# Gated attention and MLP on one core: keys on GpSimd's queue, SP in text order, and six-head turns at the end of the attention

## The chip, the core and the metric

The kernel runs on one core of one Trainium2 chip. A core has five engines with queues of their own: TensorE (PE: matmuls; PEld is its weight load), VectorE (DVE), ScalarE (ACT), GpSimd (POOL) and SyncE (SP), which here only issues DMAs. DMAs issued by SP and by GpSimd move data between HBM and the on-chip memory. Matmul results land in eight PSUM banks of 128 partitions by 512 fp32 numbers. The metric is the device time of one execution in microseconds (us); lower is better.

## What is computed

The input x has 2048 tokens of 448 features. Two blocks are computed from the same x and mixed per token by a gate:

```python
qkv = x @ wqkv                       # 16 heads of 28
p = softmax(q @ k.T * 28 ** -0.5)    # per head, 2048 x 2048
a = (p @ v) @ wo
y = layernorm(x)
b = gelu(y @ w1 + b1) @ w2 + b2      # 448 -> 1792 -> 448
g = sigmoid((x * gate_w).sum(-1))
out = g * a + (1 - g) * b
```

## The kernel before

Precision: most fp32 products are made from a high and a low part (`wh`/`wl`, `xh`/`xl`, `hl[:,0]`/`hl[:,1]`, ...). ACT copies the high part, DVE or POOL subtracts it from the raw value to get the low part, and three matmuls (high-high, high-low, low-high) go into one bank.

The work has three stages.

1. The projection stage (lines 138 to 301). For each of four token chunks `c` of 512, seven feature tiles `qk_tile(c, m)` of q and k and four token tiles `v_tile` are made. Each q/k tile is evicted by ACT (L190) and DVE (L191) into one of three buffers `hl` and stored to the HBM array `qk` (L192, 512 KB). Each value tile is evicted by ACT (L206) into one of three buffers `vt` and stored to `vs` (L208). Between these, the LayerNorm of the first chunk is prepared for the MLP (`ln_fetch`, `ln_apply`: two POOL operations, ACT's L131, one more POOL operation), and in chunk 3 the first seven tiles of w1 are loaded (L95) and split (L100, L103). In this stage only PE runs in the order of the text; for SP, ACT, DVE and POOL a planner chooses the order, and may let instructions of the next stage pass those of this one.

2. The MLP stage (from L557). For each chunk, 14 tiles `mlp1(c, f)` (11 matmuls at L529, two gelus at L532 and L533 on ACT, a subtraction on POOL at L534), then four tiles `mlp2(c, i)` (42 matmuls at L542, L543, L547). `mlp1` uses banks 0 and 1 in turn, so tile f needs the gelus of tile f-2 to be done. In chunk 0 the other seven tiles of w1 and all of w2 are fetched through four staging buffers, copied by ACT and subtracted: `low_w1` by POOL (L103), `low_w2` by DVE (L113). Between the MLP's matmuls a `filler` puts "row maxima": score matmuls of 28 rows (L362) into banks 2 to 7, whose maximum DVE takes (L342, L344). They give the softmax its shift. They read the keys of four heads, `khr` (L425, four DMAs of 224 KB), and queries `qd` (L319). Here all engines run in text order.

3. The attention stage (from L751). The 16 heads are four groups of four; 16 steps `n` = (group, chunk), each with 16 key tiles of four heads, 1024 "heads" (units) in all. They go in turns of U = 5 units: a triple of score products into banks 0 to 2 (nine matmuls, L483), an exponential of 1536 columns on ACT (L488), a pair into banks 3 and 4 and its exponential, then the value products (`pv_mm`, L746, four units to a step of four) of the key tiles that are complete, into bank 7. The units of a triple sit in different 32-row strips of PE. Up to three row-maximum matmuls per turn go into banks 5 and 6. When all 1040 row-maximum pieces are done, the turns go on without them. After each step but the last `finish` normalises the result in pieces at turns `STEPS` after the step's end; for the last group it ends with four projections (`project`, twelve matmuls at L651 to L653 in bank 6).

SP issues its DMAs in order: an issue that waits for a semaphore holds up all behind it.

Of the kernel before, what the change touches and what calls it, by code (L numbers as in the profile page):

```python
# [15 lines left out]
P = 128  # L16
S = 2048
# [17 lines left out]
W1, W2 = 0.233, 0.205  # L35
LQ = 12
STEPS = (2, 5, 7, 8, 9, 10)


@with_exitstack  # L40
def kernel(ctx: ExitStack, tc: tile.TileContext, xt, wqk, wv, wo, xk, w1, b1, w2, b2,
# [67 lines left out]
    def high_w2(f):  # L109
        nc.scalar.activation(w2h[f], wraw[2, f], AF.Copy)  # L110

    def low_w2(f):
        nc.vector.tensor_sub(w2l[f], wraw.pop((2, f)), w2h[f].bitcast(F32))  # L113

    yh, yl = (my.tile([P, n, CH], F32R, name=f"y{n}") for n in (4, 3))
    lnr = my.tile([P, 2, CH], F32, name="lnr")
# [10 lines left out]
    def ln_apply(c, t):  # L127
        x = lnx.pop((c, t))
        nc.gpsimd.tensor_sub(x, x, lnr[:, 0])
        nc.gpsimd.tensor_mul(x, x, lnr[:, 1])  # L130
        nc.scalar.activation(yh[:, t], x, AF.Copy)  # L131
        if t < 3:
            nc.gpsimd.tensor_sub(yl[:, t], x, yh[:, t].bitcast(F32))
        else:
            nc.gpsimd.tensor_sub(yh[64:128, t], x[64:128], yh[64:128, t].bitcast(F32))


    with tc.tile_pool(name="qx", bufs=2) as qx, tc.tile_pool(name="qo", bufs=3) as qo, \
# [106 lines left out]
            split_x(0, t)  # L245
        load_wqk(1)
        for c in range(NC):
            for m in range(NM):
                if c == 0:
                    if m + 2 < NM:  # L250
                        load_wqk(m + 2)
                    if m == 1:
                        for v in vt:
                            nc.gpsimd.memset(v[:, :, DH:DH + 1], 1.0)
                            nc.gpsimd.memset(v[:, :, DH + 1:32], 0.0)
                    if m == 3:
# [160 lines left out]

    khi = dict.fromkeys(range(MLP_G + 1), khr)

    def load_khr(g, k=None):  # L420

        sl = slice(0, S) if k is None else slice(k * CH, (k + 1) * CH)
        for j in range(4):
            r = D + (4 * g + j) * DH
            nc.sync.dma_start(khr[32 * j:32 * j + DH, sl].bitcast(F32), qk[0, r:r + DH, sl])  # L425

    def load_khi(g):
        if g == MLP_G:
# [40 lines left out]
        nc.sync.dma_start(qs[n][0][DH:P:32].bitcast(F32), ms[g][:, c * CH:(c + 1) * CH])  # L469

    U, UA = 5, 3
    probs = {}

    def scores(units, most, tiles):

        def product(u, i):
# [4 lines left out]
            nc.tensor.matmul(bank[:, u % U], a[r, k * P:(k + 1) * P], b[r], start=(i == 0), stop=(i == 2))  # L483

        def exps(units):
            t = tiles(len(units))
            b = units[0] % U
            nc.scalar.activation(t, bank[:, b:b + len(units)], AF.Exp, scale=SCALE)  # L488
            for i, u in enumerate(units):
                probs[u] = t[:, i]  # L490

        first, last = units[:UA], units[UA:]
        if most > 0:
            filler.max.issue(5, 1, [(first[0] + 3) % 4])
        for i in range(3):
            for u in first:
                product(u, i)
        exps(first)
        for i in range(3):
            for u in last:  # L500
                product(u, i)
            if i == 0 and most > 1:
                filler.max.issue(6, 1, [(first[0] + 1) % 4, (first[0] + 2) % 4])
        if last:
            exps(last)
        if most > 2:
            filler.max.issue(5, 1, [(first[0] + 1) % 4, (first[0] + 2) % 4])


    ml = ExitStack()  # L510
# [43 lines left out]
        nc.sync.dma_start(gbs[c * TPC + i], gb)  # L554

    E = mybir.EngineType
    with tc.manual_schedule(engines={E.SP, E.Pool, E.Activation, E.DVE}):  # L557

        order = [x for i in range(7) for x in (NF + 7 + i, i)] + list(range(7, NF))
        def high(k):  # L560
# [2 lines left out]
        def low(k):  # L563
            low_w2(k) if k < NF else low_w1(k - NF, nc.gpsimd)

        def stage(f):

            return order[max(0, 3 * (f - 1) // 2 - 1):max(0, 3 * f // 2 - 1)]

        for c in range(NC):  # L570
            for f in range(NF):
                if c == 0:
                    if f == 0:
                        stages += [lnr[:, 0], lnr[:, 1]]
# [12 lines left out]
            if c == 0:  # L587
                for k in stage(NF - 1):
                    low(k)
                for k in order[3 * (NF - 1) // 2 - 1:]:  # L590
                    high(k)
                    low(k)
                stages[2:] = []
            if c == NC - 1:
                m0.close()
# [4 lines left out]
                def early(n):  # L600
# [150 lines left out]
    with tc.manual_schedule(engines={E.SP, E.Pool, E.Activation, E.DVE}):  # L751
# [2 lines left out]
        ready = 0  # L754
        at = -1
        since = 0
        for u in range(0, 4 * steps, U):
            units = list(range(u, min(u + U, 4 * steps)))
            while at < units[-1] // 4:
                at += 1  # L760
                n, k = divmod(at, NT)
# [34 lines left out]
            ready = (units[-1] + 1) // 4  # L796
            since += 1
            if ended:
                n = summed // NT - 1
                fin, since = finish(n // NC, n % NC, pv), 0  # L800
                next(fin)
            elif fin is not None and since in STEPS:
                next(fin, None)
        while summed < steps:
            pv_mm(summed)
            summed += 1
# [54 lines left out]
```

## Time and profile before

| | us |
|---|---|
| median of 3 runs (lowest, highest) | 1138.23 (1138.23, 1141.04) |
| the profiled execution's own time | 1140.1 |
| its span, first to last instruction | 1138.3 |
| PE busy | 1114.2 |
| DVE busy | 739.6 |
| ACT busy | 633.9 |
| POOL busy | 327.2 |

Times in the profile are microseconds from the start of the span. A row of the timeline gives the start, the busy time, the engine, the line of the kernel, the operation, what it writes and reads, the count of merged instructions, and in brackets the idle time before it and who ended it. A row of the windows gives busy time (and count) of PE, PEld, DVE, ACT and POOL in a stretch, then PE's granted clock, the busy share of the DMA engines and the rate in GB/s. SPq is SP's queue of DMA issues.

### The profile page before, as it was taken

The page shows a single profiled execution, that of the slowest core. Times are in us where ns is not written, and L with a number is a line of the kernel's source. Part 1 is how long each engine was busy: PE and PEld are TensorE (multiplying, and loading weights), DVE is VectorE, ACT ScalarE, POOL GpSimd, SP SyncE. Part 2 cuts the span into 40 slices and gives each one's busy share as a digit, 9 for nine tenths or more (in the row PEclk, how much of TensorE's full clock was granted, in tenths as well). Part 3 has the DMA queues.
Part 4 walks back from the last instruction along what each step waited for, and adds up shares of the span by engine and source line. Part 5 has one row for each costly group of instructions (what it writes and reads, how often), then busy time and mean ns, then how long its engine had stood idle before and what let it go on. Part 6 is the DMA issues. An engine that isn't in the chain of part 4 may idle for free.

```text
span 1138.3 us, 19785 instructions
## 1 busy us (share of the span) xinstructions
PE 1114.2 (98%) x8136; PEld 678.9 (60%) x8136; DVE 739.6 (65%) x1031; ACT 633.9 (56%) x668; POOL 327.2 (29%) x348
## 2 busy tenths in 40 slices
PE   7999799999999999999999999999999999999996
PEld 6888677777767777744444444444444444464554
DVE  4443298888888888576666666666766766644102
ACT  5333460231131142188787887877878787747652
POOL 4006373344333332013112221221222125425140
PEclk9999899999999999999999999999999999999998
DMA  7996542010220105063100220012111102021201
GB/s 235 302 302 231 203 119 72 26 46 18 67 54 18 43 9 128 28 161 90 28 18 19 61 73 18 20 27 52 48 34 36 28 13 89 12 64 39 67 26 41
DMA packets 53055, 84.35 MB, mean 74 GB/s; under 512 B 8492, under 2 KB 28476, under 8 KB 52052
## 3 DMA queue, kind: packets, MB, share of 16 engines
q1 hardware_dynamic: 48900, 77.19, 22.5%
q0 software_dynamic: 4064, 5.89, 2.2%
q8 instruction: 64, 1.05, 0.4%
q14 instruction: 27, 0.22, 0.1%
HBM read 56.40 MB, written 26.49 MB: 73 GB/s over the span
## 4 chain that ended last, share of the span: by engine, by line
PE 94%; DMA 2%; DVE 1%; ACT 1%; issue 0%; SPq 0%; POOL 0%; ACTq 0%; DVEq 0%
PE bank L746 22%; PE bank L483 21%; PE bank L362 15%; PE bank L529 12%; PE bank L188 6%; PE bank L547 4%; PE bank L542 4%; PE bank L543 4%; PE bank L204 2%; PE bank L651 1%; PE bank L652 1%; PE bank L653 1%; DMA qk<-hl 1%; DMA raw<-in_xt 0%; DVE mx L344 0%
## 5 line engine op out<-in xcount | busy, mean ns | idle before, releaser
L488 ACT ACTIVATE pt<-bank 128x1536 f32<-128x1536 f32 (+1 forms) x408 | 482.3, 1234 | 151.5 <-PE bank L483 142.6
L342 DVE TENSOR_REDUCE mx<-bank 128x1 f32<-128x512 f32 x618 | 409.7, 687 | 175.5 <-PE bank L362 162.7
L746 PE MATMUL bank<-pt,vg 128*32 128x512 f32 x2038 | 260.9, 602 | 0.0
L344 DVE TENSOR_REDUCE mx<-bank 128x2 f32<-128x1024 f32 x203 | 238.8, 1219 | 32.5 <-PE bank L362 32.5
L362 PE MATMUL bank<-khi,qd 28*128 28x512 f32 x512 | 240.7, 479 | 0.1
L362 PEld LDWEIGHTS bank<-khi,qd 28*128 28x128 f32 x512 | 92.3, 181 | 148.1 <-DVE mx L342 105.0
L483 PE MATMUL bank<-qh,klo 28*128 28x512 f32 x1024 | 177.5, 393 | 0.0
L529 PE MATMUL bank<-y,w1f 128*128 128x512 f32 x616 | 154.1, 401 | 6.4 <-ACT h L533 6.4
L483 PE MATMUL bank<-qh,khi 29*128 29x512 f32 x768 | 160.0, 480 | 0.2 <-ACT pt L488 0.2
L529 PEld LDWEIGHTS bank<-y,w1f 128*128 128x128 f32 x616 | 113.5, 190 | 42.1 <-issue 12.3
L483 PE MATMUL bank<-ql,khi 28*128 28x512 f32 x768 | 132.3, 390 | 0.0
L534 POOL TENSOR_TENSOR hl<-h,hh 128x512 fp32r<-128x512 f32 x56 | 73.1, 1307 | 133.7 <-ACT h L533 93.0
L746 PEld LDWEIGHTS bank<-pt,vg 128*32 128x32 f32 x2038 | 45.5, 108 | 84.1 <-issue 83.3
L483 PEld LDWEIGHTS bank<-qh,klo 28*128 28x128 f32 x1024 | 89.1, 185 | 4.1
L532 ACT ACTIVATE hh<-bank,b1s 128x512 fp32r<-128x512 f32 x56 | 38.6, 689 | 88.3 <-PE bank L529 88.2
L553 ACT ACTIVATE h<-bank 128x448 f32<-128x448 f32 x16 | 8.7, 546 | 141.5 <-PE bank L547 107.5
L547 PE MATMUL bank<-w2h,hl 128*128 128x448 f32 x224 | 85.6, 382 | 0.0
L483 PEld LDWEIGHTS bank<-qh,khi 29*128 29x128 f32 x768 | 62.2, 181 | 37.6 <-ACT pt L488 33.0
L542 PE MATMUL bank<-w2h,hh 128*128 128x448 f32 x224 | 84.0, 375 | 0.0
L667 POOL DMA_DIRECT2D lt<-ob x15 | 11.0, 736 | 252.3 <-DVE ob L666 252.3
L543 PE MATMUL bank<-w2l,hh 128*128 128x448 f32 x224 | 82.5, 368 | 0.0
L362 PE MATMUL bank<-khr,qd 28*128 28x512 f32 x512 | 79.8, 466 | 1.5 <-DVE mx L344 1.5
(113 smaller groups left out, 1243.7 us busy)
## 6 DMA issues: line engine op xcount, KB each, us to landing
qk<-hl SPq DMA_DIRECT2D x28, 512.0 KB
raw<-in_xt SPq DMA_DIRECT2D x16, 256.0 KB
vs<-vt SPq DMA_DIRECT2D x16, 256.0 KB
s<-in_xt SPq DMA_DIRECT2D x16, 256.0 KB
rc<-rls POOLq DMA_DIRECT2D x60, 64.0 KB, 2.2
bxr<-in_xk SPq DMA_DIRECT2D x8, 448.0 KB
gbs<-h SPq DMA_DIRECT2D x16, 224.0 KB
klo<-qk SPq DMA_DIRECT2D x16, 224.0 KB
```

The source lines that it names most:

```text
L188: nc.tensor.matmul(ps, a, b, start=(i == 0), stop=(i == len(ops) - 1))
L342: nc.vector.reduce_max(self.mx[:, c0:c0 + 1], bank[:, b0], axis=AX)
L344: nc.vector.reduce_max(self.mx[:, c0:c1 + 1:c1 - c0], bank[:, b0:b1 + 1], axis=AX)
L362: nc.tensor.matmul(bank[:, b], self.qds[self.n][r, i * P:(i + 1) * P], khi[self.n // NC][r, k * 512:(k + 1) * 512], start=True, stop=True)
L483: nc.tensor.matmul(bank[:, u % U], a[r, k * P:(k + 1) * P], b[r], start=(i == 0), stop=(i == 2))
L488: nc.scalar.activation(t, bank[:, b:b + len(units)], AF.Exp, scale=SCALE)
L529: nc.tensor.matmul(ps, a, b, start=(i == 0), stop=(i == len(ops) - 1))
L534: nc.gpsimd.tensor_sub(hl[f], h, hh[f].bitcast(F32))
L542: nc.tensor.matmul(a, hh[f][:, sl], w2h[f], start=(f == 0), stop=False)
L543: nc.tensor.matmul(a, hh[f][:, sl], w2l[f], start=False, stop=False)
L547: nc.tensor.matmul(a, hl[f][:, sl], w2h[f], start=False, stop=(f == NF - 1))
L746: nc.tensor.matmul(pv[32 * j:32 * j + 32, :], vg[n // NC][:, k, 32 * j:32 * j + 32], probs.pop(4 * step + j), start=(k == 0), stop=(k == N ...
```

## The change

There are four parts.

- SP is put in text order from the last chunk of the projection stage on (before: from the start of the MLP stage).
- The keys `khr` of the first group are loaded on GpSimd's queue, called one `mlp1` tile earlier in the text (f = 0 instead of 1).
- At the end of chunk 0 of the MLP, the last three high parts of w2 are made first, and of the last four `low_w2` the second and fourth go to GpSimd instead of VectorE.
- In the attention, once all row maxima are done, turns have six units (two triples, banks 0 to 5), and the value products that are ready go between the two triples, except those of the last complete key tile. The second triple's exponentials go into three tiles that held keys (`khi0`, `khr`, `khi2`). The pieces of `finish` come at turns `LSTEPS`.

```diff
+LSTEPS = (2, 4, 6, 7, 8, 9)
...
-    def low_w2(f):
-        nc.vector.tensor_sub(w2l[f], wraw.pop((2, f)), w2h[f].bitcast(F32))
+    def low_w2(f, lo=nc.vector):
+        lo.tensor_sub(w2l[f], wraw.pop((2, f)), w2h[f].bitcast(F32))
...
         for c in range(NC):
+            if c == NC - 1:
+                texts.enter_context(tc.manual_schedule(engines={mybir.EngineType.SP}))
...
-    def load_khr(g, k=None):
+    def load_khr(g, k=None, queue=nc.sync):
...
-            nc.sync.dma_start(khr[32 * j:32 * j + DH, sl].bitcast(F32), qk[0, r:r + DH, sl])
+            queue.dma_start(khr[32 * j:32 * j + DH, sl].bitcast(F32), qk[0, r:r + DH, sl])
...
-    with tc.manual_schedule(engines={E.SP, E.Pool, E.Activation, E.DVE}):
+    with texts, tc.manual_schedule(engines={E.Pool, E.Activation, E.DVE}):
...
-                    if f == 1:
-                        load_khr(0)
+                    if f == 0:
+                        load_khr(0, queue=nc.gpsimd)
...
-                for k in stage(NF - 1):
-                    low(k)
-                for k in order[3 * (NF - 1) // 2 - 1:]:
+                rest = order[3 * (NF - 1) // 2 - 1:]
+                for k in rest:
                     high(k)
-                    low(k)
+                for n, k in enumerate(stage(NF - 1) + rest):
+                    low_w2(k, nc.gpsimd if n % 2 else nc.vector)
...
         exps(first)
+        if between:
+            between()
...
-        for u in range(0, 4 * steps, U):
-            units = list(range(u, min(u + U, 4 * steps)))
+        while u < 4 * steps:
+            if not late and filler.done >= NG * NC * 65:
+                late = [(mpool.tile([P, S], F32, name="khr", bufs=1) if g == MLP_G else
+                         aq.tile([P, S], F32, name=f"khi{g}")) for g in range(NG - 1)]
+            units = list(range(u, min(u + (UL if late else U), 4 * steps)))
...
+            def values(upto):
+                nonlocal summed, ended
+                while summed < upto and not ended:
+                    pv_mm(summed)
+                    summed += 1
+                    ended = summed % NT == 0
+
+            def pt(n, p):
+                if late and p:
+                    late.append(late.pop(0))
+                    return late[-1][:, :n * CH].rearrange("p (n c) -> p n c", c=CH)
+                return ap.tile([P, n, CH], F32, name=f"pt{n}")
+
             if u:
-                scores(units, min(3, filler.due()), lambda n: ap.tile([P, n, CH], F32, name=f"pt{n}"))
-            ended = False
-            while summed < ready and not ended:
-                pv_mm(summed)
-                summed += 1
-                ended = summed % NT == 0
+                scores(units, min(3, filler.due()), pt, (lambda: values(ready - 1)) if late else None)
+            values(ready)
```

In the changed program the orders of the engines near the end of the projection stage are these. SP issues the seven `qk` stores of chunk 3, each followed by one load (the LayerNorm's fourth input tile after the first, then w1 tiles), then the four `vs` stores, then the `qd` loads, then the staged weight loads. Before, three of the four `qd` loads stood ahead of the first of these stores, the fourth `qd` load, three staged weight loads and the first `khr` load between them, and the other `khr` loads between the `vs` stores or right behind them. ACT evicts the first three q/k tiles of chunk 3 before the first split of w1 and before the fourth LayerNorm copy, and the other four in turn with w1 splits. Before, all seven stood behind the fourth LayerNorm copy. POOL issues the four `khr` loads between the w1 subtractions of tiles 2, 4 and 5.

More of the change, by code (lines that the diff above doesn't have):

```diff
@@ L135, in ln_apply @@
             nc.gpsimd.tensor_sub(yh[64:128, t], x[64:128], yh[64:128, t].bitcast(F32))
+    texts = ExitStack()
     with tc.tile_pool(name="qx", bufs=2) as qx, tc.tile_pool(name="qo", bufs=3) as qo, \
@@ L471, with scores, product @@
     U, UA = 5, 3
+    UL = 6
     probs = {}
-    def scores(units, most, tiles):
-        def product(u, i):
+    def scores(units, most, tiles, between=None):
+        def product(p, i):
+            u = units[p]
             n, k, j = u // 4 // NT, u // 4 % NT, u % 4
@@ L482, in product, with exps @@
             r = slice(32 * j, 32 * j + r)
[L483 to L492, printed above, removed]
+            nc.tensor.matmul(bank[:, p], a[r, k * P:(k + 1) * P], b[r], start=(i == 0), stop=(i == 2))
+        def exps(at):
+            t = tiles(len(at), at[0])
+            nc.scalar.activation(t, bank[:, at[0]:at[-1] + 1], AF.Exp, scale=SCALE)
+            for i, p in enumerate(at):
+                probs[units[p]] = t[:, i]
+        first, last = list(range(len(units)))[:UA], list(range(len(units)))[UA:]
         if most > 0:
-            filler.max.issue(5, 1, [(first[0] + 3) % 4])
+            filler.max.issue(5, 1, [(units[0] + 3) % 4])
         for i in range(3):
-            for u in first:
-                product(u, i)
+            for p in first:
+                product(p, i)
         exps(first)
+        if between:
+            between()
         for i in range(3):
-            for u in last:
-                product(u, i)
+            for p in last:
+                product(p, i)
             if i == 0 and most > 1:
-                filler.max.issue(6, 1, [(first[0] + 1) % 4, (first[0] + 2) % 4])
+                filler.max.issue(6, 1, [(units[0] + 1) % 4, (units[0] + 2) % 4])
         if last:
@@ L506, in scores @@
         if most > 2:
-            filler.max.issue(5, 1, [(first[0] + 1) % 4, (first[0] + 2) % 4])
+            filler.max.issue(5, 1, [(units[0] + 1) % 4, (units[0] + 2) % 4])
     ml = ExitStack()
@@ L598, with early @@
                 first = {3: aq.tile([P, S], F32, name="klo", bufs=2), 2: aq.tile([P, NT, P], F32, name="vg", bufs=2)}
-                def early(n):
+                def early(n, p):
                     t = first[n] if n == 3 else first[n].rearrange("p a b -> p (a b)")
@@ L756 @@
         since = 0
-        for u in range(0, 4 * steps, U):
-            units = list(range(u, min(u + U, 4 * steps)))
+        u = 0
+        late = []
+        while u < 4 * steps:
[3 more added lines that the diff above has]
+            units = list(range(u, min(u + (UL if late else U), 4 * steps)))
             while at < units[-1] // 4:
@@ L788 @@
                         load_v(g + 1)
-            if u:
-                scores(units, min(3, filler.due()), lambda n: ap.tile([P, n, CH], F32, name=f"pt{n}"))
-            ended = False
-            while summed < ready and not ended:
-                pv_mm(summed)
-                summed += 1
-                ended = summed % NT == 0
+            ended = False
+            def values(upto):
[9 more added lines that the diff above has]
+                return ap.tile([P, n, CH], F32, name=f"pt{n}")
+            if u:
+                scores(units, min(3, filler.due()), pt, (lambda: values(ready - 1)) if late else None)
+            values(ready)
             ready = (units[-1] + 1) // 4
@@ L799 @@
                 n = summed // NT - 1
-                fin, since = finish(n // NC, n % NC, pv), 0
+                fin, since, when = finish(n // NC, n % NC, pv), 0, LSTEPS if late else STEPS
                 next(fin)
-            elif fin is not None and since in STEPS:
+            elif fin is not None and since in when:
                 next(fin, None)
+            u = units[-1] + 1
         while summed < steps:
```

## The prediction

> **What bounds the kernel now.** I read the page's busy lines and slices first, then the chain, then the timelines of PE, ACT, SP and DVE where the slices of PE dip.
>
> ```profile
> span 1138.3 us, 19785 instructions
> PE 1114.2 (98%) x8136; PEld 678.9 (60%) x8136; DVE 739.6 (65%) x1031; ACT 633.9 (56%) x668; POOL 327.2 (29%) x348
> PE   7999799999999999999999999999999999999996
> PE 94%; DMA 2%; DVE 1%; ACT 1%; issue 0%; SPq 0%; POOL 0%; ACTq 0%; DVEq 0%
> ```
>
> TensorE is busy 98% of the span and 94% of the chain. So a change helps in two ways only: it fills a hole of PE, or it takes PE work away. Leaving out the first and last slices, which the change does not touch, the one dip is the fifth slice, 114 to 142 us.
>
> ```profile
> 117.25 5.18 PE L529 MATMUL bank<-y,w1f 128*128 128x512 f32 x22
> 128.59 4.29 PE bank L529 x11
> 122.40:128.60 6.20, 0.04 (x2) 0.01 (x1) 0.16 (x1) 3.15 (x5) 0.00 (x0) 0.71 0.97 343
> 128.60:132.90 4.30, 4.30 (x12) 3.44 (x13) 0.85 (x1) 2.08 (x4) 2.52 (x2) 0.63 0.48 103
> ```
>
> PE does the MLP's first two tiles (22 matmuls from 117.25, 0.235 us each) to 122.42 and then stands until 128.59: 6.17 us. The third tile's 11 matmuls then take 4.29 us instead of 11 x 0.235 = 2.59, at a clock of 0.63: 1.70 us more. Who held PE? The third tile needs bank 0, so the first gelu. ACT's and SP's rows before it:
>
> ```profile
> 102.82 0.63 ACT L131 ACTIVATE y<-s 128x512 fp32r<-128x512 f32 x1 [4.73 <-POOL s L130]
> 105.34 0.59 ACT L190 ACTIVATE hl<-bank 128x512 fp32r<-128x512 f32 x1
> 116.67 0.60 ACT L190 ACTIVATE hl<-bank 128x512 fp32r<-128x512 f32 x1 [3.89 <-DMA qk<-hl]
> 119.61 1.41 ACT L206 ACTIVATE vt<-bank 128x448 f32<-128x448 f32 x3
> 125.42 0.54 ACT L206 ACTIVATE vt<-bank 128x448 f32<-128x448 f32 x1 [4.39 <-DMA vs<-vt]
> 125.98 1.28 ACT L532 ACT_TABLE_LOAD   x1
> 119.03 0.32 SPq L425 DMA_DIRECT2D khr<-qk  x1
> 122.66 1.12 SPq L425 DMA_DIRECT2D khr<-qk  x1
> ```
>
> ACT begins the seven evictions of chunk 3 only at 105.34, behind the LayerNorm copies. With three buffers they run at the pace of the stores (waits on the DMA). The last value eviction waits for a store to 125.42; the table load and two gelus follow. From there to PE's start it is 128.59 - 125.42 = 3.17 us. SP meanwhile issues key loads between the stores.
>
> **Part by part.**
>
> *SP in text order, keys on GpSimd.* In the changed order three q/k evictions and two value evictions stand right behind ACT's third LayerNorm copy, and SP issues no staged weight load and no `qd` load before the last value store. When does the last value eviction start?
>
> ```profile
> 97.02 0.63 ACT L131 ACTIVATE y<-s 128x512 fp32r<-128x512 f32 x1 [4.04 <-POOL s L130]
> 105.00:110.00 5.00, 5.00 (x24) 4.29 (x23) 4.03 (x6) 2.72 (x6) 2.76 (x2) 1.00 0.62 213
> 110.00:115.00 5.00, 5.00 (x27) 4.58 (x26) 1.70 (x3) 0.90 (x2) 0.00 (x0) 1.00 1.01 323
> qk<-hl SPq DMA_DIRECT2D x8, 512.0 KB
> raw<-in_w SPq DMA_DIRECT2D x4, 256.0 KB
> khr<-qk SPq DMA_DIRECT2D x4, 224.0 KB
> ```
>
> The third copy ends at 97.65; two value evictions (about 0.5 each) and a q/k eviction with its subtraction bring the first store to about 99.5. From there to the store that the last eviction waits for, 7 x 512 KB go to `qk`, 7 x 256 KB come from w1, one 256 KB LayerNorm tile and the first 256 KB value store move, and two key loads of 224 KB: 6336 KB, 6.5 MB. At 323 to 343 GB/s (the stretches with a DMA share near 1) that takes 19 to 20 us, to 118.5 to 119.6. At 213 GB/s it is 30.5 us, to 130.0. I take 120.5, one us behind the first, since the DMA engines were only 0.62 busy at the low rate: there they lacked work. PE then goes on at 120.5 + 3.17 = 123.7: gain 4.9. Best: the gelu is there by 122.42, gain 6.17. Worst: 133.2, a loss of 4.6. Of the slow third tile's 1.70 us I take half, 0.85: a hole of 1.3 us is left, and the second part's rows show a low clock after holes of that size. Sum 5.75.
>
> What is queued behind the new waits: POOL's key loads wait for the q/k stores of tiles 3 and 4, and the w1 subtractions of tiles 4 and 5 and the first gelu subtraction stand behind them. Tile 4 starts some 5 us after the third (two tiles of 2.59), near 129; the keys are wanted there too, and with ACT's last w1 split near 118 the last key load is issued by about 120. Some 6 us are left, so I cost this at nothing. SP's `qd` and staged loads come about 2 us after the last value store, 123 to 125, before the third tile's gelu (126). Nothing.
>
> *Subtractions of w2 on GpSimd at the end of chunk 0.*
>
> ```profile
> 168.65 1.41 DVE L113 TENSOR_TENSOR w2l<-lnr,w2h 128x448 fp32r<-128x448 f32 x2
> 169.98 1.15 DVE L113 TENSOR_TENSOR w2l<-s,w2h 128x448 fp32r<-128x448 f32 x2
> 173.45 0.50 PE L362 MATMUL bank<-khr,qd 28*128 28x512 f32 x2 [0.43 <-DVE mx L344]
> 174.58 0.50 PE L362 MATMUL bank<-khr,qd 28*128 28x512 f32 x2 [0.64 <-DVE mx L344]
> 175.10:180.10 5.00, 5.00 (x17) 4.32 (x17) 2.82 (x3) 0.00 (x0) 2.55 (x2) 0.66 0.13 46
> 167.76 1.28 POOL L534 TENSOR_TENSOR hl<-h,hh 128x512 fp32r<-128x512 f32 x1 [0.55 <-ACT h L533]
> L113 DVE TENSOR_TENSOR w2l<-s,w2h x7: 610/625/1708, 137.2 to 170.5; 128x448 fp32r<-128x448 f32 x7
> ```
>
> DVE's four subtractions take 168.65 to 171.05, 2.40 us; the maxima behind them are late, PE waits 0.43 + 0.64 = 1.07 us, and the low clock costs 5.0 x 0.34 = 1.7. Two subtractions fewer at 0.61 are 1.2 us: then the 1.07 and perhaps the 1.7 go. But an L113 also takes 1.708 us. If the two left take that beside POOL's, 3.4 us, the maxima come 1.0 later and PE loses 1.0. The first of the four already ran beside POOL's L534 of 167.76; now POOL's two follow at once. I take 1.05 each, 2.1 us: gain 0.3.
>
> The Trainium skill, page "SBUF — State Buffer", section "Who interferes with whom", says that a DVE instruction with two SBUF inputs contends with a GpSimd instruction that reads SBUF: it speaks against this part. By it DVE's two and POOL's two run one after the other, and the gain is about nothing.
>
> The Trainium skill, page "TensorE: Matmul & The Clock Gate", section "HAM oscillation", has PE throttled by idle gaps above about 3.4 us. By it the hole of 1.3 us that I leave in the transition keeps the clock, the whole 1.70 is gained there, and that part's sum is 6.6. The rows above do not agree: 1.07 us of holes are followed by a clock of 0.66, though the matmuls between them use 28 rows only.
>
> *Six-head turns.*
>
> ```profile
> 1043.86 0.52 PE L483 MATMUL bank<-qh,khi 29*128 29x512 f32 x4
> 1060.34 0.53 PE L483 MATMUL bank<-qh,khi 29*128 29x512 f32 x4
> 1061.94 1.06 PE L746 MATMUL bank<-pt,vg 128*32 128x512 f32 x8
> 1069.96 1.92 PE L746 MATMUL bank<-pt,vg 128*32 128x512 f32 x16
> 1071.82 0.53 PE L483 MATMUL bank<-qh,khi 29*128 29x512 f32 x4
> 1077.21 0.51 PE L483 MATMUL bank<-qh,khi 29*128 29x512 f32 x3
> 1077.92 0.50 PE L483 MATMUL bank<-qh,khi 29*128 29x512 f32 x2
> 1078.82 1.06 PE L746 MATMUL bank<-pt,vg 128*32 128x512 f32 x8
> 1079.81 0.50 PE L483 MATMUL bank<-qh,khi 29*128 29x512 f32 x3
> 1080.71 0.50 PE L483 MATMUL bank<-qh,khi 29*128 29x512 f32 x2
> 1115.30 2.78 PE L746 MATMUL bank<-pt,vg 128*32 128x512 f32 x24
> ```
>
> Turns without row maxima run from 1043.86 to 1115.30: 89 heads in 17 turns of five and one of four. Now they are 14 of six and one of five. A five-head turn's scores take 1060.34 to 1061.94 = 1.60 us: the triple and the pair are six passes of about 0.24, since the heads of a group run beside each other on different rows. Two triples are six passes too. So three turns' scores go, 3 x 1.60 = 4.8. Against this: in seven turns a value step lies between the triples, and the first triple then drains, 0.90 (1079.81 to 1080.71) instead of 0.71 (1077.21 to 1077.92): 7 x 0.2 = 1.4. And four double value steps (1069.96 to 1071.82, 1.86) become two single ones (1078.82 to 1079.81, 0.99 each): 4 x 0.12 = 0.5. PE waits for exponentials little in both; I credit 0.2 for the pair's drain that goes. Sum 3.1. Upper end: also all five such waits of 0.2 to 0.3, so 6. Lower end: turns without projection gain nothing, 1.5.
>
> The new exponential tiles held keys last read long before; no wait. The projection comes six turns after the step's end, later in time than before or equal, since turns are longer: nothing.
>
> Sum: 5.75 + 0.3 + 3.1 = 9.15. The profiled execution took 1140.1 (span 1138.3 and 1.8 around it); less 9.15 that is 1130.95. It stands 1.9 above the median of the runs, 1138.23; against that the forecast is 1129.1.
>
> **Rivals.**
>
> *All holes close.* 6.17 + 1.70, 1.07 + 1.7 and 6.0: 16.6, so 1121.6. For it: the 343 GB/s of the full stretch; against it: DVE and POOL side by side.
>
> *The transition stays DMA-paced.* The stores leave earlier, but w1 loads now stand between them, so the last eviction stays near 125.4; only the tail gains: 1138.2 - 3.4 = 1134.8. For it: ACT's waits on the stores; against it: DMA shares of 0.6 where the stores waited for ACT.
>
> *Slower by the same mechanism.* If the 6.5 MB move at 190 GB/s, the last eviction comes at 133.7, PE at 136.9, 8.3 later: 1138.2 + 8.3 - 3.4 = 1143.1. It decides from an eviction at about 129 on. Only the low-share stretches are near that rate.
>
> *It does nothing:* ACT's third copy is late by as much as the new order saves, and the six-head turns wait for exponentials: 1138.
>
> **The numbers.** Forecast 0.60, all holes close 0.15, DMA-paced 0.12, slower 0.07, nothing 0.06. A measurement tells 0.3%, 3.4 us, from no change. DMA-paced lies on that bound; I count 0.11 of it as faster. Faster 0.86, same 0.07, slower 0.07. The range takes in the closing of all holes and the DMA-paced case: 1121.5 to 1135.
>
> **What would show it.** Right: the first q/k eviction of chunk 3 near 98 instead of 105, the last value eviction near 120, a hole of PE below 2 us before the third tile; L113 rows above 1 us beside POOL's at the end of chunk 0; 15 turns from the end of the row maxima to the last value products, in about 68 us instead of 71.4. Wrong: a hole of more than 5 us there, PE waiting for keys at the first row maxima, or PE waits on ACT's exponentials in the late turns.

## The result, and the profile after

The changed kernel takes 1127.38 us (median of 6 runs, 1125.63 to 1129.43) against 1136.14 us (6 runs, 1133.22 to 1141.04): ratio 0.9914, 95% interval 0.9896 to 0.9932 (the quotient of the two medians, 0.9923, lies inside it). The forecast was 1129.1. The size is right; where it comes from is not what was forecast.

The page of the changed kernel: the span, the busy line, PE's slices and the chain.

```profile
span 1125.7 us, 19775 instructions
PE 1107.3 (98%) x8136; PEld 673.6 (60%) x8136; DVE 734.1 (65%) x1029; ACT 634.3 (56%) x662; POOL 331.5 (29%) x354
PE   7999799999999999999999999999999999999998
PE 84%; DMA 7%; POOL 3%; DVE 2%; ACT 1%; issue 1%; SPq 1%; ACTq 0%; POOLq 0%; DVEq 0%
```

The fifth slice still has its dip, and the last slice went from 6 to 8, which nobody had expected. Four marks that both traces have divide the span: the first reduction of row maxima (DVE, `mx`), the first and the last `mf` (DVE folds a finished tile of maxima), and the last output row on DVE. The timeline of DVE and, in a second fence, the windows at the end of the span (columns as in the prediction; the last number is GB/s), first of before:

```profile
139.96 3.49 DVE L344 TENSOR_REDUCE mx<-bank 128x2 f32<-128x1024 f32 x3 [1.42 <-PE bank L362]
190.94 0.22 DVE L378 TENSOR_REDUCE mf<-mx 128x16 f32<-128x64 f32 x1
1042.38 0.22 DVE L378 TENSOR_REDUCE mf<-mx 128x16 f32<-128x64 f32 x1
1127.12 2.51 DVE L658 SCALAR_TENSOR_TENSOR klo<-bank,gate,klo 128x448 f32<-128x448 f32 x4 [0.94 <-PE bank L653]
```

```profile
1131.00:1132.00 1.00, 0.00 (x0) 0.00 (x0) 0.00 (x0) 0.00 (x0) 0.00 (x0) 0.95 0.14 50
1132.00:1138.30 6.30, 0.00 (x0) 0.00 (x0) 0.00 (x0) 0.00 (x0) 0.00 (x0) 0.50 0.00 0
```

The same two of after:

```profile
139.66 3.49 DVE L350 TENSOR_REDUCE mx<-bank 128x2 f32<-128x1024 f32 x3 [1.43 <-PE bank L368]
189.19 0.22 DVE L384 TENSOR_REDUCE mf<-mx 128x16 f32<-128x64 f32 x1
1039.11 0.22 DVE L384 TENSOR_REDUCE mf<-mx 128x16 f32<-128x64 f32 x1
1120.00 2.52 DVE L667 SCALAR_TENSOR_TENSOR klo<-bank,gate,klo 128x448 f32<-128x448 f32 x4 [0.94 <-PE bank L662]
```

```profile
1124.00:1125.70 1.70, 0.00 (x0) 0.00 (x0) 0.00 (x0) 0.00 (x0) 0.00 (x0) 1.00 0.03 8
```

| stretch of the profiled execution | before, us | after, us | gain |
|---|---|---|---|
| start to the first row maximum | 139.96 | 139.66 | 0.30 |
| from there to the first `mf` | 50.98 | 49.53 | 1.45 |
| from there to the last `mf` | 851.44 | 849.92 | 1.52 |
| from there to the end of the last output row on DVE | 87.25 | 83.41 | 3.84 |
| from there to the end of the span | 8.67 | 3.18 | 5.49 |
| sum | 1138.3 | 1125.7 | 12.6 |

The transition, forecast at 5.75, gave 0.30. The largest piece is the last: the kernel before ends about 7 us after its last transfer, with no engine busy and nothing moving; the changed one ends 1.6 us after it. The profiled pair is 12.6 us apart, the medians 8.8, so part of this account is scatter of single executions.

Why did the transition stay? ACT, POOL, PE and SP after (timelines; the PE row is the third MLP tile and what follows it up to the first row maxima):

```profile
94.96 1.09 ACT L193 ACTIVATE hl<-bank 128x512 fp32r<-128x512 f32 x2
103.16 0.63 ACT L101 ACTIVATE w1f<-raw 128x512 fp32r<-128x512 f32 x1 [5.78 <-DMA raw<-in_w]
118.64 0.63 ACT L101 ACTIVATE w1f<-raw 128x512 fp32r<-128x512 f32 x1 [5.12 <-DMA raw<-in_w]
123.31 0.96 ACT L209 ACTIVATE vt<-bank 128x448 f32<-128x448 f32 x2
110.36 1.29 POOL L431 DMA_DIRECT2D khr<-qk  x2 [0.85 <-DMA qk<-hl]
119.36 1.29 POOL L104 TENSOR_TENSOR w1f<-raw,w1f 128x512 fp32r<-128x512 f32 x1 [7.71 <-DMA raw<-in_w]
126.90 12.27 PE L538 MATMUL bank<-y,w1f 128*128 128x512 f32 x40 [5.70 <-ACT h L542]
119.73 5.89 SPq L211 DMA_DIRECT2D vs<-vt  x4
```

The evictions of chunk 3 start at 95, earlier than forecast. But in ACT's program the w1 splits stand between the evictions, which come behind them: the splits wait for w1 loads, which SP issues behind 512 KB stores. Of these waits ACT has five, 17.0 us together. Meanwhile GpSimd sends for the keys from 110.36 on, ahead of the value stores. The last value eviction ends at 124.27 instead of 125.96, and the hole of PE is 5.70 us instead of 6.17. (The third tile itself starts 1.69 us earlier, since the MLP begins earlier too; where most of that was lost again is told with the prediction below.) Which of the two holds it, the w1 loads or the keys, is what the experiments ask.

### The profile page after: what moved, and what is told of

It reads as the page before. It is cut to its first block, busy times and chain, and to the rows that moved or that the text cites. A ratio compares the mean times of both kernels' runs of the same rounds, so it can differ in the third digit from the quotient of the medians.

```text
span 1125.7 us, 19775 instructions
## 1 busy us (share of the span) xinstructions
PE 1107.3 (98%) x8136; PEld 673.6 (60%) x8136; DVE 734.1 (65%) x1029; ACT 634.3 (56%) x662; POOL 331.5 (29%) x354
## 3 DMA queue, kind: packets, MB, share of 16 engines
q8 instruction: 64, 1.05, 0.4%
## 4 chain that ended last, share of the span: by engine, by line
PE 84%; DMA 7%; POOL 3%; DVE 2%; ACT 1%; issue 1%; SPq 1%; ACTq 0%; POOLq 0%; DVEq 0%
PE bank L755 22%; PE bank L491 20%; PE bank L368 15%; PE bank L538 11%; PE bank L556 4%; PE bank L551 4%; PE bank L552 4%; DMA raw<-in_xt 2%; DMA bxr<-in_xk 1%; PE bank L660 1%; DMA raw<-in_w 1%; PE bank L661 1%; PE bank L662 1%; POOL hl L543 1%; DMA s<-in_xt 1%
## 5 line engine op out<-in xcount | busy, mean ns | idle before, releaser
L495 ACT ACTIVATE pt<-bank 128x1536 f32<-128x1536 f32 (+1 forms) x387 | 462.1, 1244 | 141.2 <-PE bank L491 141.2
L491 PE MATMUL bank<-qh,klo 28*128 28x512 f32 x1024 | 174.7, 393 | 0.0
L491 PE MATMUL bank<-qh,khi 29*128 29x512 f32 x768 | 157.3, 480 | 0.0
L491 PE MATMUL bank<-ql,khi 28*128 28x512 f32 x768 | 129.7, 390 | 0.0
```

Of the source, the lines that this page charges most:

```text
L491: nc.tensor.matmul(bank[:, p], a[r, k * P:(k + 1) * P], b[r], start=(i == 0), stop=(i == 2))
L495: nc.scalar.activation(t, bank[:, at[0]:at[-1] + 1], AF.Exp, scale=SCALE)
```

## The experiments

Every kernel below computes the whole result. This table has the marks of one profile each: the hole of PE ahead of the MLP's third tile, the time of the first row maximum, the two stretches that have a part of the change in them, and the time from the last landing to the end of the span, in us.

| kernel | hole | first row maximum | to first `mf` | last `mf` to last output row | idle end |
|---|---|---|---|---|---|
| before | 6.17 | 139.96 | 50.98 | 87.25 | 7.1 |
| pad8 | 5.55 | 139.50 | 49.77 | 87.22 | 7.1 |
| lows | 6.10 | 141.85 | 49.73 | 86.89 | 7.1 |
| six | 5.53 | 140.28 | 51.64 | 83.47 | 7.1 |
| sp_only | 3.50 | 136.68 | 49.96 | 87.19 | 7.1 |
| khr_only | 8.14 | 142.49 | 49.53 | 86.88 | 1.6 |
| q_order | 8.69 | 140.82 | 51.90 | 87.18 | 1.5 |
| after | 5.70 | 139.66 | 49.53 | 83.41 | 1.6 |
| after_again | 8.12 | 141.31 | 49.75 | 83.44 | 1.6 |
| early_w1 | 2.27 | 135.61 | 49.73 | 83.41 | 1.6 |
| khr_late | 2.88 | 134.12 | 52.52 | 83.40 | 1.6 |
| early_khr | 0.17 | 132.46 | 51.41 | 83.42 | 1.6 |
| dma4 | 2.48 | 134.75 | 51.54 | 86.93 | 1.3 |
| pad64 | 6.97 | 144.57 | 49.77 | 86.93 | 7.1 |

**The parts, each alone** (q_order, lows, six), and the changed kernel again beside them.

q_order is before with SP's text order and the keys on GpSimd's queue:

```diff
+            if c == NC - 1:
+                texts.enter_context(tc.manual_schedule(engines={mybir.EngineType.SP}))
-                    if f == 1:
-                        load_khr(0)
+                    if f == 0:
+                        load_khr(0, queue=nc.gpsimd)
```

> The queue part alone: SyncE in text order from chunk 3 on and the key loads on GpSimd's queue; the w2 subtractions and the turns of five heads stay as before. The prediction priced this part at 5.75 us, so by it the ratio to the kernel before is near 0.995. The changed kernel's trace has only 0.08 us of lead left where the second matmuls of the mlp's first chunk begin (166.22 and 166.14 us), so my present theory expects 0 to 0.5 us, a ratio of 0.9995 to 1.000, with the TensorE hole ahead of the mlp's third tile at 5 us or more. The third reading, that text order by itself costs something that the other parts hid, expects a ratio above 1.001.

Measured: 1134.13 us, ratio 0.9965 (0.9953 to 0.9977). None of the three readings fits. The gain is there, but in the profile the last output row is later than before (1131.47 against 1129.63) and the hole grew to 8.69 us; the 5.5 us come from the end of the span.

lows is before with the w2 part:

```diff
-                    low(k)
+                for n, k in enumerate(stage(NF - 1) + rest):
+                    low_w2(k, nc.gpsimd if n % 2 else nc.vector)
```

> The w2 part alone: the last four w2 subtractions behind the roundings and divided between VectorE and GpSimd. The prediction priced it at 0.3 us, a ratio of 0.9997. In the two traces the lead grew by 1.68 us over this stretch (0.08 us at 166, 1.76 us at 179), of which 1.5 us is a stretch of low granted clock that the kernel before has at 175 to 180 us and the changed kernel has not. If that low clock goes because of this part, the ratio here is near 0.9985 and this run's profile shows full clock from 170 to 185 us; if it is chance in which kernel's holes fall where, the profile may show it again and the ratio is 0.999 to 1.001.

Measured: 1137.63 us, ratio 0.9986 (0.9972 to 1.0000), and the profile has full clock here. That looks like the first reading, but pad8, sp_only, khr_only and pad64 have the subtractions of before, and full clock too. The low clock near 176 us is in four of the eight profiles without this part (before, six, q_order, dma4) and in none of the six with it: whether the part keeps it away or chance did, stays open. Where the clock is full throughout, the stretch takes 49.53 to 49.96 us without the part and 49.53 to 49.75 with it: the subtractions themselves give nothing that shows. (khr_late and early_khr have a low clock earlier in that stretch.)

six is after with the queues and the w2 subtractions of before, so the six-head turns alone (the diff of that part stands above the prediction).

> The turns of six heads alone, with the value products between their triples; queues and w2 subtractions as before. The prediction priced it at 3.1 us (ratio 0.9973), with ends of 1.5 and 6. The two traces give 3.9 us from the start of the late turns to the copy behind the last one (74.36 and 70.49 us), a ratio of 0.9966. If the smaller drift of 1.4 us that the changed kernel gains between the mlp and the late turns also comes from this part, the ratio is 0.995; if that drift belongs to the queue part, it stays at 0.9966.

Measured: 1136.52 us, ratio 0.9982 (0.9967 to 0.9997), and 83.47 us from the last `mf` to the last output row. In all six kernels with these turns that stretch takes 83.40 to 83.47 us, in all eight without them 86.88 to 87.25: a gain of 3.4 to 3.9 us, the firmest number of this study. The interval leaves out both ratios that were expected, 0.9966 by a hair. The other drift, between the MLP and the late turns, is not this part's: from the first `mf` to the last, six takes 851.55 us, before 851.44.

> The changed kernel itself, unchanged, on the same chip as its three parts: ratio 0.9914 expected as measured before. If the parts add, their three differences sum to this one's; a rest over 0.2% (about 2 us) would mean that they act on one another. The span in the profile is expected to end 2 to 7 us after the last output has landed, and this piece to differ from run to run with no kernel work in it.

Measured: 1127.37 us, ratio 0.9903 (0.9881 to 0.9924). The three parts alone gave 0.35, 0.14 and 0.18%, together 0.67%, against 0.97% here. The rest of 0.30% is over the bound that I had set, but the half widths of the four intervals, 0.12 to 0.22% each, come to 0.32% as the root of the sum of their squares; whether the parts act on one another stays open. The end of the span was expected to differ from run to run; it is 1.6 us again.

**The keys, the order, or the length of GpSimd's program?** khr_only moves the keys alone, sp_only SP's order alone, pad8 adds eight writes:

```diff
+    padt = const.tile([P, 8], F32, name="padt")
+    for i in range(8):
+        nc.gpsimd.memset(padt[:, i:i + 1], 0.0)
```

> The kernel before with one move: the four key loads of the first group go through GpSimd's queue, at the start of the mlp's first chunk; SyncE stays as it was. Three kernels whose GpSimd has 352 to 354 instructions on the profile's page end 1.6 to 1.9 us after the last output has landed, three with 348 to 350 end 7 us after it, so 5.5 us of the gain may hang on GpSimd's instruction count alone. Theory A, the length of GpSimd's program decides that end: here it has 352, so the end is short, and with the loads' order nearly without effect the ratio is 0.995 to 0.996. Theory B, SyncE's text order shortens the end: the end stays at 7 us and the ratio is 0.999 to 1.001. The hole ahead of the mlp's third tile should stay near 6 us, since the stores and their loads stand as before. Beside theory A stands a rule of the Trainium skill, page Runtime: NRT & Kernel Launch, section Instruction fetch mechanics: a branch to code outside the pages that are already held waits until they are fetched.

Measured: 1134.00 us, ratio 0.9983 (0.9963 to 1.0004). The end is short, as theory A has it, but the ratio stays above its 0.995 to 0.996: the hole did not stay near 6 us, it grew to 8.14, and the first row maximum came 2.5 us later than before.

> The kernel before with SyncE in text order from chunk 3 on; the key loads stay on SyncE, so GpSimd keeps 348 or 349 instructions. Theory A (GpSimd's program length): the end stays at 7 us after the last landing, and the ratio shows the order alone, 0.999 to 1.002. Theory B (SyncE's text order): end of 1.6 to 1.9 us, ratio 0.995 to 0.997. For the order alone: ScalarE waits for w1 loads that stand behind the 512 KB stores, as in the changed kernel (17 us in 5 waits there), and the TensorE hole ahead of the third mlp tile is 5 to 9 us.

Measured: 1135.96 us, ratio 0.9987 (0.9967 to 1.0006). The end is long. The hole is 3.50 us, not the 5 to 9 expected here, though ACT waits 14.2 us for w1 loads: the order alone (with the order that the planner then chooses for ACT) does most of what the prediction forecast of it, and the first row maximum comes at 136.68. Four kernels with the order of before (before, pad8, lows, six) have it at 139.50 to 141.85, mean 140.4: 3.7 us gained. Three with order and early keys (after, after_again, q_order) have 139.66 to 141.31, mean 140.6: the keys take 3.9 us back. The starts of the third tile say the same, 128.5 us in the mean of the four, 128.7 in the three, 124.85 here. This is one profile of sp_only, and two of the changed kernel lie 1.65 us apart, so I trust the price to a microsecond or two. Timelines of PE, SP and ACT in sp_only:

```profile
124.85 10.98 PE L533 MATMUL bank<-y,w1f 128*128 128x512 f32 x40 [3.50 <-ACT h L537]
122.65 1.73 SPq L323 DMA_DIRECT2D qd<-qk  x4
125.83 1.69 SPq L429 DMA_DIRECT2D khr<-qk  x4
116.68 0.47 SPq L95 DMA_DIRECT2D raw<-in_w  x1
120.72 0.63 ACT L100 ACTIVATE w1f<-raw 128x512 fp32r<-128x512 f32 x1 [1.04 <-DMA raw<-in_w]
```

The last two rows are the last w1 load of the stage and ACT's split that waits for it, 4.0 us later. The same two in the changed kernel lie 8.0 us apart:

```profile
114.80 1.05 SPq L96 DMA_DIRECT2D raw<-in_w  x1
122.78 0.63 ACT L101 ACTIVATE w1f<-raw 128x512 fp32r<-128x512 f32 x1 [1.19 <-DMA raw<-in_w]
```

The keys are issued here at 125.83, behind all stores, and the row maxima still start 3 us earlier than in the changed kernel, whose keys go out from 110.36 on. They were never late. On GpSimd's own queue they only came early, and the w1 loads, already issued by SP, landed later beside them: from the last one to its split it is 8.0 us in after and in after_again and 7.6 in q_order, 4.0 in sp_only and 3.6 in khr_late below, where the keys follow the value stores.

> The kernel before with eight writes of one column of a small spare tile added at the start of GpSimd's program, and nothing else: no order, no load, no turn is changed. Theory A (GpSimd's program length decides the end): 356 instructions, the span ends 1.6 to 1.9 us after the last output has landed instead of 7.2, and the ratio is 0.995 to 0.996, as large a gain as the whole queue part had. Theory B or any cause in the queues: end of 7 us, ratio 1.000 within 0.15%.

Measured: 1135.42 us, ratio 0.9992 (0.9969 to 1.0016), end long. So eight more plain instructions on GpSimd do not shorten the end; with khr_only and sp_only what is left is the keys' move to GpSimd's queue. Theory A as I wrote it fell.

**Repairs of the transition.** early_w1 is after with the w1 tiles fetched ahead of the stores:

```diff
                 if c == 3:
-                    fetch_w1(m, raw())
+                    if m < 3:
+                        fetch_w1(m + 4, raw())
...
+                if c == 2:
+                    fetch_w1(i, raw())
```

> The changed kernel with w1 tiles 0 to 3 fetched in chunk 2's value tiles and 4 to 6 behind chunk 3's first three q/k stores, so that ScalarE's roundings of w1 no longer wait for loads behind the 512 KB stores. Theory 1 (those waits make the hole): the five waits of ScalarE for raw, 17.0 us in the changed kernel, shrink below 5 us, the last value copy moves from 123.8 us to about 119, and the hole ahead of the third mlp tile from 5.0 to under 3 us. Theory 2 (the 6.5 MB of transfers set the end whatever waits for what): the waits move to the stores' buffers and the hole stays at 4 us or more. For the time, theory 3 says that VectorE, busy 29.5 of 30 us between 140 and 170, gives nothing on: the second matmuls of the first mlp chunk still begin near 166.1 us and the ratio stays at that of the changed kernel, 0.990 to 0.992; if a closed hole is kept, the ratio is 0.986 to 0.989.

Measured: 1124.54 us, ratio 0.9903 (0.9874 to 0.9931; the runs of before lie wide here, 1131.04 to 1140.81). The hole is 2.27 us; the last value eviction begins at 120.96 (PE and ACT in early_w1):

```profile
124.14 10.98 PE L541 MATMUL bank<-y,w1f 128*128 128x512 f32 x40 [2.27 <-ACT h L545]
120.96 0.55 ACT L209 ACTIVATE vt<-bank 128x448 f32<-128x448 f32 x1 [5.79 <-DMA vs<-vt]
```

ACT's waits for these w1 tiles fell from 17.0 us in five to 6.2 in two, not quite below the 5 expected, and the last eviction now waits for a value store. Theory 1 holds against theory 2. Theory 3 fell: the first `mf` comes at 185.34 instead of 189.19. VectorE paces that stage, but the stage begins with the first row maximum and takes its 49.7 us from there, so a lead at its start is kept.

khr_late is after with the keys behind the value stores, early_khr has both repairs:

```diff
-                    if f == 0:
+                    if f == 1:
                         load_khr(0, queue=nc.gpsimd)
```

> The changed kernel with its four key loads one tile later in GpSimd's program, behind the first tile's subtraction, so that they start behind the value stores instead of 9 to 16 us ahead of the last of them. Theory: the early key loads (0.9 MB) take the transfer time of the stores and w1 loads that the end of the projection waits for; text order without them had a hole of 3.5 us and the third mlp tile at 124.85 us, with them 5.7 to 8.7 us and 126.9 to 129.6. So here: hole 3.5 us or less, third tile at 125 us or earlier, first 16-row maximum at 187 us or earlier (189.2 and 191.1 in the changed kernel's two profiles), end of span 1.6 us after the last landing, ratio 0.987 to 0.989. Rival: the queue that carries the keys makes no difference to the transition and the difference between the profiles is scatter from run to run; then hole 5 to 8 us and ratio 0.990 to 0.992.

Measured: 1125.72 us, ratio 0.9894 (0.9877 to 0.9912); hole 2.88 us, third tile at 124.24, first `mf` at 186.64. The theory holds by these marks, and the rival's hole of 5 to 8 us does not come; the interval of the ratio takes in both. Part is given back: the row maxima are now early enough to wait for the keys, 1.01 us (PE in khr_late):

```profile
124.24 9.38 PE L538 MATMUL bank<-y,w1f 128*128 128x512 f32 x40 [2.88 <-ACT h L542]
135.52 0.50 PE L368 MATMUL bank<-khr,qd 28*128 28x512 f32 x3 [1.01 <-DMA khr<-qk]
```

> Both repairs together: w1 tiles fetched ahead of the stores as before in the run early_w1, and the key loads behind the value stores. If the two causes are separate and both cost transfer time, the hole ahead of the third mlp tile is under 2 us (2.27 with the w1 tiles moved alone), that tile starts by 123 us, the first 16-row maximum stands by 184.5 us, and the ratio is 0.985 to 0.987. If only one can be earned because the remaining transfers then bind, it stays at the time of early_w1, 1124.5 us, within 1 us.

Measured: 1123.96 us, ratio 0.9880 (0.9862 to 0.9897), the fastest of all, 3.4 us below the median of the changed kernel in its own runs. The hole is closed, and the first row maximum comes 8 us before that of the four kernels with the old order. Two marks of early_khr, PE and ACT:

```profile
121.82 9.37 PE L541 MATMUL bank<-y,w1f 128*128 128x512 f32 x40 [0.17 <-ACT h L545]
118.64 0.55 ACT L209 ACTIVATE vt<-bank 128x448 f32<-128x448 f32 x1 [3.05 <-DMA vs<-vt]
```

The rows say that the gain was to be had. The time does not: it lies 0.6 us below that of early_w1, within the 1 us of the second reading, and the ratio is above the 0.985 to 0.987 of the first. How much each repair has beside the other the times do not tell, since they lie within 1.8 us of one another.

**The end of the span.** dma4 is before with four tiny transfers from GpSimd, pad64 is pad8 with 64 writes:

```diff
+    for i in range(4):
+        nc.gpsimd.dma_start(padt[:, 2 * i:2 * i + 2], b1[:, :2])
```

> The kernel before with four tiny transfers (two columns of the bias, 1 KB each) issued by GpSimd at its start; nothing else is moved, so GpSimd issues 131 transfers as in the runs with the keys on its queue, instead of 127. Theory A2 (four more transfers issued by GpSimd shorten the end, whatever they carry): the span ends 1.6 us after the last landing instead of 7.1, ratio 0.994 to 0.997. Theory A3 (it is the keys' own place or SyncE's four fewer transfers): the end stays at 7.1 us and the ratio at 1.000 within 0.2%.

> The kernel before with 64 writes of a spare column at the start of GpSimd's program, 28 ns each, in a stretch where GpSimd waits 3 us for its first operand. Eight such writes left the end at 7.1 us. If the length of GpSimd's program decides the end and a transfer is only worth many plain instructions, the end falls to 1.6 us here; if the number of transfers issued by GpSimd decides it, the end stays at 7.1 us and the ratio is 1.000 within 0.2%.

Measured: dma4 1128.15 us, ratio 0.9918 (0.9902 to 0.9934), pad64 1141.69 us, ratio 1.0034 (1.0018 to 1.0050). In both the added instructions also changed the order that the planner chose for the projection stage, which I had not intended, so these times are not the price of the additions alone: the first row maximum comes at 134.75 in the one and at 144.57 in the other. The end of the span is not touched by that. The windows there, of dma4 and then of pad64:

```profile
1124.00:1125.00 1.00, 0.00 (x0) 0.00 (x0) 0.00 (x0) 0.00 (x0) 0.00 (x0) 1.00 0.90 335
1125.00:1126.30 1.30, 0.00 (x0) 0.00 (x0) 0.00 (x0) 0.00 (x0) 0.00 (x0) 1.00 0.00 0
```

```profile
1132.00:1133.00 1.00, 0.00 (x0) 0.00 (x0) 0.00 (x0) 0.00 (x0) 0.00 (x0) 1.00 0.99 373
1133.00:1140.20 7.20, 0.00 (x0) 0.00 (x0) 0.00 (x0) 0.00 (x0) 0.00 (x0) 0.60 0.00 1
```

So four more transfers issued by GpSimd, whatever they carry and wherever they stand, take 5.5 us off the end: all eight profiles with them end 1.3 to 1.6 us after the last landing, all six without them 7.1. Why, no run shows. The program of before has 127 transfers from GpSimd, these have 131; where between them the border lies, and whether it is a count of transfers or something that they add to GpSimd's program, was not tried. The Trainium skill, page "Runtime: NRT & Kernel Launch", section "Instruction fetch mechanics", has a branch wait for code that is not held. No run here shows such a wait: in the idle stretch the DMA engines move next to nothing (the windows above), the pages of all fourteen profiles list the same instruction queues, 64 and 27 packets, and 64 plain instructions did not move the end. Also open: of the kernel before only one execution was profiled, so whether each of its runs (1131.04 to 1142.22 over all sessions) has the long end is not known.

## Why the prediction was right, and where it was wrong

*The total was right for the wrong reason, by luck.* 9.15 us were forecast; the medians differ by 8.8. The transition's 5.75 hardly came, and 5.5 us at the end of the program, in no term of the sum, took their place. By the prediction's own sign its first part was wrong: the hole is above 5 us.

*"The last value eviction ... I take 120.5."* The last two run from 123.31 to 124.27. The first eviction was forecast near 98 and came at 94.96, so the start was not what failed. Two steps failed. The first is the last step of that part, "some 6 us are left, so I cost this at nothing", said of the keys on GpSimd: I asked whether they would be late, not what they displace. sp_only shows the price, 3.9 us, and khr_late that it can be had back. The second is the treatment of the w1 loads as mere bytes: ACT's splits wait for each in turn, and the evictions stand behind the splits. early_w1 and early_khr show what that costs: with both mended the hole is 0.17 us. The rate was too high as well: from 96.3 to 123.3 us the changed kernel's DMA engines moved 263 GB/s at a busy share of 0.82, not 323 to 343. The order alone (sp_only) earned 3.7 of the 5.75.

*"Of the slow third tile's 1.70 us I take half."* The loss grew instead. PE's row of before beside that of after above:

```profile
128.59 10.88 PE L529 MATMUL bank<-y,w1f 128*128 128x512 f32 x40 [6.17 <-ACT h L533]
```

The same 40 matmuls take 10.88 us before and 12.27 after. So of the 1.69 us by which the third tile starts earlier, 1.39 are lost behind it, and the 0.30 of the account are left. The windows of 115 to 145 us, first before and then after, have the same mean granted clock, 0.89:

```profile
115.00:145.00 30.00, 23.56 (x101) 18.15 (x101) 9.16 (x13) 16.31 (x29) 11.40 (x9) 0.89 0.54 183
115.00:145.00 30.00, 24.30 (x99) 18.59 (x98) 8.55 (x12) 17.84 (x30) 15.47 (x14) 0.89 0.58 192
```

What differs is where the low clock lies. In windows of a quarter of a microsecond it is 0.50 for 6.8 us in both. Before, it begins near 125.0, and 3.6 us of it fall into the hole, where they cost nothing; after, it begins near 126.3, and only 0.6 us do.

*w2 subtractions, 0.3.* They gave about nothing. DVE and POOL at the end of chunk 0, after:

```profile
168.78 0.66 DVE L114 TENSOR_TENSOR w2l<-lnr,w2h 128x448 fp32r<-128x448 f32 x1
169.37 1.57 DVE L114 TENSOR_TENSOR w2l<-s,w2h 128x448 fp32r<-128x448 f32 x1
170.87 6.87 DVE L350 TENSOR_REDUCE mx<-bank 128x2 f32<-128x1024 f32 x6
168.91 1.54 POOL L114 TENSOR_TENSOR w2l<-lnr,w2h 128x448 fp32r<-128x448 f32 x1
170.42 1.53 POOL L114 TENSOR_TENSOR w2l<-s,w2h 128x448 fp32r<-128x448 f32 x1
```

The prediction took 1.05 us for each of DVE's two; they took 0.66 and 1.57, the second beside POOL's, and the maxima begin at 170.87 instead of 171.05. By the rule of the Trainium skill that spoke against this part (page "SBUF — State Buffer", section "Who interferes with whom") the gain is about nothing: the trace agrees. The 1.7 us of low clock that this part "perhaps" removes is absent after, but also in four kernels that lack the part.

*Six-head turns, 3.1.* Right in mechanism, 0.3 to 0.8 too small: 3.4 to 3.9. The turns themselves were sized well: from their first score product to the last value products they took 71.44 us before (1043.86 to 1115.30) and take 68.45 after (1040.59 to 1109.04), 3.0 us less. What the sum lacks stands behind them, the last value products, on the chain of before and after:

```profile
1115.37 2.71 PE bank L746 x24
```

```profile
1109.11 1.85 PE bank L755 x16
```

24 matmuls stand behind the last exponential before and 16 after, 0.86 us: the sum ended where they start and left them out. The waits of PE for exponentials did not grow into a cost: one of 0.2 us in these turns before, none after.

*The rivals.* "The transition stays DMA-paced" (0.12) came nearest in its place, hole above 5 us, but its 1134.8 lacked the end of the program. "It decides from an eviction at about 129 on", the slower case, was not reached: in q_order, the worst of this order, the last eviction began at 126.42.

## What to carry to other kernels

That nobody waits for a load does not make it free to move it to an idle queue: ask which transfers it now runs beside or ahead of. When evictions and splits share an in-order engine, the loads of the splits belong ahead of the stores of the evictions. And when a total comes out right, divide the two traces at marks that both have before believing the sum.

## What the runs showed of the hardware that was not expected

The span can go on for 7.1 us after the last transfer has landed, with every engine idle, and four more transfers issued by GpSimd, even 1 KB each, make that 1.3 to 1.6 us.

The granted clock drops to half speed in pieces of 3.41 us, and the hole does not set their number alone. Added up in windows of a quarter of a microsecond, the stretches of low clock between 112 and 190 us are 3.4 us in five of the fourteen profiles, 6.8 in four and 10.2 in five, to within 0.02 one, two and three times 3.41. The windows of 115 to 145 us of early_w1, with a hole of 2.27 us, and of dma4, with one of 2.48:

```profile
115.00:145.00 30.00, 27.73 (x121) 21.02 (x122) 11.61 (x12) 17.05 (x29) 15.61 (x12) 0.94 0.48 161
```

```profile
115.00:145.00 30.00, 27.41 (x127) 20.79 (x126) 14.01 (x17) 19.29 (x33) 16.31 (x13) 1.00 0.57 182
```

The first has one such piece from 124.6 us on, behind its hole; the larger hole of dma4 has none, nor has that of 2.88 us in khr_late, whose piece comes at 136.2, behind its wait of 1.01 us for the keys. The Trainium skill, page "TensorE: Matmul & The Clock Gate", section "HAM oscillation", puts the limit at idle gaps of about 3.4 us; here a gap of 2.27 us was followed by the low clock, so the traces do not agree with it as a sharp limit.

From the first `mf` to the last the code is the same in all fourteen but for instructions moved ahead of it, and PE stands still there for under 1 us in all. Nine profiles took 849.8 to 850.2 us for it, five 851.4 to 851.7 (before, pad8, six, sp_only, q_order). The 1.52 us of the account are this difference. It is no single event: before and after are level at the seventh of the sixteen `mf` (261.82 and 261.79 us after the first) and draw apart over the nine behind it. No part of the change goes with it, and no row shows its cause.
